# Handing out a long convolution between the steps of a Fourier layer: half-step pieces, an inverse in two channel halves, W products on every other step

## The chip, the cores and the metric

The kernel runs on one core of one Trainium2 chip. The metric is the device time of one execution in microseconds (us); smaller is better. Five engines work side by side: TensorE (PE in the profile, with its weight loads as PEld), VectorE (DVE), ScalarE (ACT), GpSimd (POOL), and SyncE (SP), which here issues DMAs and nothing else. Each engine runs its own instructions strictly in order.

## The reference

The input x has 2048 rows and 576 channels. Four layers follow each other, A, B, A, B, each added to its input:

```python
x = x + _A_ref(_layernorm(x), ...)   # FNet: y = Cr @ (n @ Wr.T) - Ci @ (n @ Wi.T)
x = x + _B_ref(_layernorm(x), ...)   # H3:   y = q * (longconv(kv, ssm_k) + kv * ssm_D)
...
```

In A, `Cr`, `Ci` are the 2048x2048 Fourier matrices of the sequence and `Wr`, `Wi` the 576x576 ones of the channels. In B, `kv` is a 4-tap convolution of k times v, `longconv` is a causal convolution of 2048 taps for each channel, done by a Fourier transform of length 4096, and q is the normalized input. So the long convolution does not depend on x: it is worked out once and used by both B layers, and until the first B needs it, it can be done at any time.

## The kernel before, in words

All products are in fp32r with three terms (high x high, high x low, low x high), so every matrix is first **split** (lines 80 to 82): ACT copies the rounded high part, DVE subtracts it for the low part.

**The main row of work** is `layer` (line 275): 128 steps of 14 matmuls of 128x512, four row blocks (tb) x real and imaginary (g) x 16 contractions (k). Each step needs one 256 KB block of the Fourier matrix (`load_c`, line 189: SP load, ACT and DVE split) and one normalized block X[k]. At the end of each g the sums are split into U (`evac_u`). When both halves of a tb are there, U times W makes eight **W products** (`hidden`, line 251: 27 matmuls of 128x288 each, two for each of four row blocks jj), handed out by `finish`. W itself is loaded and split by `load_w`, three parts a step in steps 41 to 43.

**The branch** (`branch`, line 320) is the long convolution, a generator that the main loop (lines 565 to 587) advances between steps. It has three stages:

- **f1**: 32 items; each loads a block, splits it, and does 12 matmuls of 128x288, whose results go to DRAM `t_d` by ACT's DMA queue (lines 381 to 391).
- **mid**: 64 groups (2 channel halves x 32). A group loads 288 KB of `t_d` through SP, is split (`mid_split`), has a forward product of 6 matmuls into two PSUM banks (`mid_forward`), then four ACT copies (lines 429 to 432), four DVE products and sums (lines 434 to 437), a split, and two groups later an inverse product of 3 matmuls (`mid_inverse`), one ACT copy (line 448) and a store to `v_d` (line 449).
- **i2**: 16 items of two loads of 288 KB each from `v_d`, two splits, 256 KB of constants `i2c` through POOL's DMA queue (`load_fr`, line 144), 12 matmuls for both channel halves, and a store of 288 KB to `yb_d[j]` (lines 468 to 489). It begins when all 64 groups are stored, since each item reads all of them.

The number of branch items after each step is fixed by hand: f1 until step 40, mid from step 44 to 101 (64 groups in 58 steps, about 1.1 a step), i2 from step 102 to 117 (one a step). `finish(pending, 1)` gives one W product a step from step 44. From step 118 (`PREP`) `get_x1` gates and normalizes the rows for the second A layer (it needs `yb_d[j]`). The `land` ring through which the loads of mid and i2 pass has two slots of 288 KB. The matmuls of the branch and of W share three PSUM banks (`bank`, line 66). A scheduler of the framework then fixes each engine's order from the program; an engine follows that order whatever happens on the chip.

After the 128 steps the second A layer uses a scheme of its own (Strassen, line 725), which the change doesn't touch.

Of the kernel before, what the change touches and what calls it, by code (L numbers as in the profile page):

```python
# [15 lines left out]
P = 128  # L16
S = 2048
D = 576
# [15 lines left out]
MID_END = 101  # L34
I2_END = 117
PREP = 118
MID_LAG = 2
KP = 4
# [16 lines left out]
def fnet_h3_kernel(ctx: ExitStack, tc: tile.TileContext, x, c_mat, w_re, w_im, k_pad, v, shift_k,  # L55
# [95 lines left out]
    nc.vector.memset(mhalf, -0.5)  # L151

# [25 lines left out]
    v_d = dr.tile([P, J, 2, D], F32, name="vd")  # L178
# [96 lines left out]
    def layer(get_x, xres, done, pending, blocks=TB):  # L275
        steps = [(g, tb, k) for tb in range(blocks) for g in range(2) for k in range(J)]
        for n, (g, tb, k) in enumerate(steps):
# [33 lines left out]
            yield n  # L311
# [8 lines left out]
    def branch():  # L320
# [24 lines left out]
        fcs = [None, None]  # L345

        def f1_loads(j, src):
            if fcs[0] != j:
                fc = quads(ring["fc"]())
                load_fr(fc, f1c[j])  # L350
                fcs[:] = j, fc
# [8 lines left out]
            return r, fcs[1]  # L360
# [32 lines left out]
        todo = [(j, 1) for j in range(K_FIRST)] + [(j, 0) for j in range(K_FIRST)]  # L393
# [12 lines left out]
        lay(m1, 0, ("df", 2 * D, 3), ("yf", D, 3), ("mc", 4 * P, 1))  # L406
        fresh("land")
# [6 lines left out]

        def mid_split(hf, qg):
            df = parts("df")
            d = ring["land"]()
            load_after(d, t_d[hf][4 * qg:4 * qg + 4].rearrange("q j c s d -> (q j c) (s d)"))
            split(*df, d)
            return df  # L420
# [21 lines left out]
        def mid_inverse(hf, qg, yf):  # L442
# [6 lines left out]
            nc.scalar.dma_start(v_d[4 * qg:4 * qg + 4, :, :, hf * HD:(hf + 1) * HD]  # L449
                              .rearrange("q j c d -> (q j c) d"), vo)  # L450

        dfs, yfs = [], []
        groups = [(hf, qg) for hf in range(2) for qg in range(32)]
        for n in range(len(groups) + MID_LAG + 1):
            if n >= MID_LAG + 1:
                mid_inverse(*groups[n - MID_LAG - 1], yfs.pop(0))
            if 1 <= n <= len(groups):
                yfs.append(mid_forward(dfs.pop(0)))
            if n < len(groups):
                dfs.append(mid_split(*groups[n]))  # L460
            if n < len(groups):
                yield

        fresh("fc")
        lay(m1, 0, ("vf", 2 * D, 4), ("fc", 4 * P, 2))
        lay(flts, SC_AT + 3 * NT + 2 * D, ("yo", D, 2))

        def i2_split(j):
            fc = quads(ring["fc"]())
            load_fr(fc, i2c[j])  # L470
            vf = []
            for c in range(2):
                vt = ring["land"]()
                load_after(vt, v_d[:, j, c])
                vf.append(parts("vf"))
                split(*vf[c], vt)
            return fc, vf

        def i2_products(j, fc, vf):
            yo = ring["yo"]()  # L480
            for hf in range(2):
                cs = slice(hf * HD, (hf + 1) * HD)
                ps = bank()
                for c in range(2):
                    mm(ps[:, :HD], fc[:, c, :], vf[c][0][:, cs], c == 0, False)
                    mm(ps[:, :HD], fc[:, c, :], vf[c][1][:, cs], False, False)
                    mm(ps[:, :HD], fc[:, 2 + c, :], vf[c][0][:, cs], False, c == 1)
                nc.scalar.activation(yo[:, cs], ps[:, :HD], AF.Copy)
            nc.scalar.dma_start(yb_d[j], yo)

        nxt = i2_split(0)
        for j in range(J):
            yield
            i2_products(j, *nxt)
            if j + 1 < J:
                nxt = i2_split(j + 1)
# [58 lines left out]
    load_x(0)  # L555
    load_x(1)
    for used in range(1, K_FIRST + 1):
        next(br)
        if used <= 2:
# [5 lines left out]
    for n in layer(get_x0, lambda j: x[:, j, :], done0, pending):  # L565
        if n <= F1_END:
            want = K_FIRST + (F1_16 * n // 16 if n <= 16 else F1_16 + (32 - K_FIRST - F1_16) * (n - 16) // (F1_END - 16))
        elif n <= MID_END:
            want = 33 + 64 * max(0, n - W_END) // (MID_END - W_END)
        else:  # L570
            want = min(114, 97 + 17 * (n - MID_END) // (I2_END - MID_END))
        while used < want:
            next(br, None)
            used += 1
        if F1_END < n <= W_END:
            for _ in range(3):
                next(wl, 0)
        if n >= W_SAVE and n % 2 == 0:
            next(wl, 0)
        if n > W_END:  # L580
            finish(pending, 1)
# [202 lines left out]
    for n in layer(get_x1, lambda j: xb_d[j], done1, pending, 1):  # L784
# [119 lines left out]
```

## Time and profile before

| what | value |
|---|---|
| median of 3 runs | 1252.8 us (1250.85 to 1253.81) |
| the profiled execution's own time | 1250.6 us |
| its span, first to last instruction | 1248.8 us |
| PE busy | 1195.5 us, 96% of the span, 6320 matmuls |
| DVE, ACT busy | 847.2 us (68%), 657.9 us (53%) |
| DMA | 258.29 MB, mean 207 GB/s |

How to read it: "busy" of PE counts pipelined matmuls with modelled ends, so a 128x512 matmul shows 393 ns though the next one starts much earlier. What a stretch cost beyond its matmuls is better read from start times: in steps that wait for nothing, 14 matmuls of 128x512 begin every 3.18 us (683.27 to 686.45), which is 227 ns each, and 162 matmuls of 128x288 took 21.47 us (235.20 to 256.67), which is 132 ns each. Called **lost** in this document is the time of a stretch less the number of its matmuls times these two pitches. A line in the groups view has line, engine, operation, output<-input, sizes and count, then busy time, mean ns of one, and the engine's idle time before them with what ended it.

The time lost, by stretch of the profiled execution (matmul counts from the groups of each stretch):

| us from the span's start | steps, work | matmuls 512 / 288 wide | lost |
|---|---|---|---|
| 0 to 8 | before the first matmul | 0 | 8.0 |
| 8 to 222 | steps 0 to 44, f1; W arrives | 637 / 399 | 16.7 |
| 262 to 345 | mid | 241 / 167 | 6.3 |
| 392 to 600 | mid | 506 / 606 | 13.1 |
| 600 to 680 | i2 | 180 / 169 | 16.8 |
| 680 to 800 | gate, W products of tb 3, second layer's first steps | 366 / 216 | 8.4 |

The two stretches left out between (222 to 262 and 345 to 392) lost under 1 us each; they are full of W products.

### The profile page before, as it was taken

How to read it: one execution, taken by the hardware profiler on the slowest of the kernel's cores; microseconds unless marked ns; L12 is line 12 of the kernel's file. 1: busy time of each engine (PE TensorE's matmuls, PEld its weight loads, DVE VectorE, ACT ScalarE, POOL GpSimd, SP SyncE). 2: the span in 40 equal slices, each digit the busy share in tenths (PEclk: the TensorE clock that was granted, in tenths of full speed). 3: DMA queues.
4: the chain of work that ended last, by engine and by line, in shares of the span. 5: the costliest groups of instructions: out<-in, count | busy, mean ns of one | idle time of the engine just before them, and what ended most of it. 6: DMA issues, size and time to landing. Idle time of an engine off the chain costs nothing.

```text
span 1248.8 us, 18341 instructions
## 1 busy us (share of the span) xinstructions
PE 1195.5 (96%) x6320; PEld 1027.7 (82%) x6320; DVE 847.2 (68%) x1559; ACT 657.9 (53%) x1314; POOL 76.2 (6%) x102
## 2 busy tenths in 40 slices
PE   7999999999999999999898999999999999999997
PEld 5788887888799878798777797788878878879997
DVE  7999884468854887844354974566667668775674
ACT  6865655368854887744454862544444444450220
POOL 2210000000000000000100421000000000000111
PEclk9999999999999999999999999999999999999999
DMA  9989987545565555444888883675375378787631
GB/s 320 317 249 302 274 255 222 167 128 182 179 192 164 178 144 164 134 125 126 257 259 244 295 300 130 224 254 168 117 242 190 111 255 265 256 273 225 207 134 48
DMA packets 141648, 258.29 MB, mean 207 GB/s; under 512 B 15346, under 2 KB 39922, under 8 KB 141555
## 3 DMA queue, kind: packets, MB, share of 16 engines
q1 hardware_dynamic: 102674, 205.73, 51.9%
q10 hardware_dynamic: 33984, 42.48, 9.7%
q0 software_dynamic: 4896, 8.92, 3.1%
q8 instruction: 50, 0.82, 0.3%
q14 instruction: 44, 0.35, 0.1%
HBM read 190.42 MB, written 66.65 MB: 206 GB/s over the span
## 4 chain that ended last, share of the span: by engine, by line
PE 59%; DMA 15%; DVE 11%; ACT 8%; issue 5%; POOL 2%; ACTq 0%; SPq 0%; POOLq 0%; DVEq 0%
PE s L64 31%; PE bk L64 23%; PE rm L64 5%; DMA flts<-vd 5%; DMA ph<-in_c_mat 3%; DMA t<-flts 2%; DVE mats L82 1%; ACT mid L81 1%; DMA flts<-in_c_mat 1%; DVE mid L82 1%; POOL flts L513 1%; ACT mats L81 1%; DMA xa<-flts 1%; DVE flts L373 1%; DVE ph L682 1%
## 5 line engine op out<-in xcount | busy, mean ns | idle before, releaser
L64 PE MATMUL s<-mats 128*128 128x512 f32 x2094 | 528.6, 393 | 5.4 <-DVE flts L159 2.4
L64 PEld LDWEIGHTS s<-mats 128*128 128x128 f32 x2094 | 384.6, 188 | 81.4 <-DVE mats L82 6.8
L82 DVE TENSOR_TENSOR mats<-flts,mats 128x512 fp32r<-128x512 f32 x209 | 142.8, 686 | 75.2 <-ACT mats L81 72.1
L81 ACT ACTIVATE mats<-flts 128x512 fp32r<-128x512 f32 x209 | 130.2, 626 | 116.5 <-PE rm L64 71.2
L64 PE MATMUL bk<-mid 128*128 128x288 f32 x768 | 133.4, 304 | 18.3 <-ACT mid L81 9.3
L64 PEld LDWEIGHTS bk<-mid 128*128 128x128 f32 x768 | 114.3, 188 | 44.5 <-ACT mid L81 16.6
L81 ACT ACTIVATE mid<-flts 128x576 fp32r<-128x576 f32 (+1 forms) x160 | 93.8, 588 | 88.5 <-DVE flts L437 53.4
L82 DVE TENSOR_TENSOR mid<-flts,mid 128x576 fp32r<-128x576 f32 (+1 forms) x160 | 101.8, 638 | 54.5 <-ACT mid L81 51.9
L64 PE MATMUL bk<-w,u 128*128 128x288 f32 x864 | 121.9, 296 | 4.8 <-ACT w L215 1.4
L64 PEld LDWEIGHTS bk<-w,u 128*128 128x128 f32 x864 | 117.2, 188 | 8.4 <-ACT w L215 1.8
L64 PE MATMUL rm<-mats 128*128 128x512 f32 x338 | 104.8, 390 | 0.0
L64 PE MATMUL bk<-f1r 128*128 128x288 f32 x384 | 62.6, 306 | 13.2 <-ACT f1r L81 8.0
L64 PEld LDWEIGHTS rm<-mats 128*128 128x128 f32 x338 | 63.3, 188 | 13.1
L64 PEld LDWEIGHTS bk<-f1r 128*128 128x128 f32 x384 | 57.6, 195 | 19.1 <-ACT flts L390 8.1
L160 POOL TENSOR_TENSOR flts<-flts 128x1 f32<-128x1 f32 x40 | 37.5, 938 | 519.2 <-DVE flts L159 519.2
L64 PE MATMUL s<-t,mats 128*128 128x512 f32 x258 | 64.5, 389 | 0.0
L390 ACT ACTIVATE flts<-bk 128x288 f32<-128x288 f32 x128 | 47.7, 409 | 25.0 <-DMA t<-flts 15.8
L64 PE MATMUL bk<-mats 128*128 128x288 f32 (+1 forms) x340 | 56.7, 309 | 0.0
L64 PEld LDWEIGHTS s<-t,mats 128*128 128x128 f32 x258 | 48.4, 188 | 10.1
L434 DVE TENSOR_TENSOR flts<-bk,flts 128x288 f32<-128x288 f32 x64 | 29.2, 456 | 34.1 <-ACT flts L430 33.8
L64 PEld LDWEIGHTS bk<-mats 128*128 128x128 f32 x340 | 48.8, 188 | 2.0
L64 PE MATMUL s<-mats,u 128*128 128x512 f32 x198 | 49.9, 389 | 0.0
(147 smaller groups left out, 1521.5 us busy)
## 6 DMA issues: line engine op xcount, KB each, us to landing
flts<-in_c_mat SPq DMA_DIRECT2D x150, 256.0 KB, 3.7
ph<-in_c_mat SPq DMA_DIRECT2D x48, 512.0 KB, 4.0
t<-flts ACTq DMA_DIRECT2D x64, 288.0 KB, 4.4
flts<-t SPq DMA_DIRECT2D x64, 288.0 KB, 2.9
flts<-in_c_mat SPq DMA_DIRECT2D x36, 512.0 KB, 4.9
vd<-flts ACTq DMA_DIRECT2D x64, 144.0 KB, 3.2
flts<-vd SPq DMA_DIRECT2D x32, 288.0 KB, 3.6
ud<-ph ACTq DMA_DIRECT2D x12, 512.0 KB, 4.8
```

The costliest lines, as they stand in the source:

```text
L64: nc.tensor.matmul(ps, lhsT, rhs, start=first, stop=last, skip_group_check=more)
L81: nc.scalar.activation(h, src, AF.Copy)
L82: nc.vector.tensor_tensor(l, src, h.bitcast(F32), OP.subtract)
L160: pows.append(nc.gpsimd.tensor_tensor(rs, ve, mhalf, OP.pow).ins)
L373: nc.vector.tensor_tensor(tmp if t else r, kr[j + t], w, OP.mult)
L390: nc.scalar.activation(so[:, c, :], ps[:, :HD], AF.Copy)
L434: nc.vector.tensor_tensor(p1, px[:, :HD], p1, OP.mult)
L513: pows.append(nc.gpsimd.tensor_tensor(rs, sv, mhalf, OP.pow).ins)
L682: nc.vector.tensor_tensor(src, src, r, OP.add)
```

## The change

- **Order of W products.** `finish(pending, 1)` is called on every second step instead of each (three in steps 44 to 46 as before).
- **Branch by TensorE time.** From step 44 to 111 the branch is handed out in proportion to the TensorE time of the steps (3.2 us a step, 3.6 us a W product), with each branch piece reporting a cost (0.4 and 2.7 for the two parts of a mid group, 1.2 for an i2 item; sum 236.8), and it may also be advanced in the middle of a step (`layer` yields twice). f1's last item comes one step earlier.
- **Inverse in two channel halves.** `v_d` is two tensors. i2 has 32 items of half the channels: one 288 KB load, one split, 6 matmuls, a store of 144 KB; each loads its 256 KB of `i2c` anew. The first half's items start between the groups of the second half (from group 37, every second one, until 4 are left), the other 20 come after the last group. A load is issued two items ahead and split one item ahead, where before load and split stood together.
- **Rings.** `yf` has 2 slots instead of 3; `fc` (the i2c blocks) 2 slots, and 2 more after the last group. `land` keeps its 2.
- **PREP** moves from 118 to 113.
- **First loads.** The x loads of blocks 0 and 1 are issued after the first f1 load instead of ahead of it, f1 starts with block 1 instead of block 0 (which needs `ssm_d` added), and a one-element activation comes ahead of the first wait, so that ACT's table load is not behind it.

```diff
-MID_END = 101
-I2_END = 117
-PREP = 118
+I2_END = 111
+PREP = 113
+I2_FIRST = 37
+I2_LATE = 4
+PIECE = 3.6
+STEP = 3.2
...
+    nc.scalar.activation(flts[:, 1:2], mhalf, AF.Copy)
...
+                if dc == NC // 2 - 1:
+                    yield n, False
...
-        todo = [(j, 1) for j in range(K_FIRST)] + [(j, 0) for j in range(K_FIRST)]
+        todo = [(j, 1) for j in reversed(range(K_FIRST))] + [(j, 0) for j in range(K_FIRST)]
...
-        lay(m1, 0, ("df", 2 * D, 3), ("yf", D, 3), ("mc", 4 * P, 1))
-        fresh("land")
+        at = lay(m1, 0, ("df", 2 * D, 3), ("mc", 4 * P, 1))
+        fresh("land", "fc")
+        spare = at
+        at = lay(m1, at, ("yf", D, 2))
+        lay(m1, at, ("fc", 4 * P, 2))
...
+        def i2_products(hf, j, fc, vf):
+            yo = ring["vo"]()
+            ps = bank()
             for c in range(2):
+                cs = slice(c * HD, (c + 1) * HD)
+                mm(ps[:, :HD], fc[:, c, :], vf[0][:, cs], c == 0, False)
+                mm(ps[:, :HD], fc[:, c, :], vf[1][:, cs], False, False)
+                mm(ps[:, :HD], fc[:, 2 + c, :], vf[0][:, cs], False, c == 1)
+            nc.scalar.activation(yo, ps[:, :HD], AF.Copy)
+            nc.scalar.dma_start(yb_d[j][:, hf * HD:(hf + 1) * HD], yo)
+
+        mids = [(0, hf, qg) for hf in range(2) for qg in range(32)]
+        late = [(1, 0, j) for j in range(J)]
+        feeds = []
+        for g, f in enumerate(mids):
+            feeds.append(f)
+            if g >= I2_FIRST and (g - I2_FIRST) % 2 == 0 and len(late) > I2_LATE:
+                feeds.append(late.pop(0))
+        feeds += late + [(1, 1, j) for j in range(J)]
...
+        for i, (kind, hf, q) in enumerate(feeds):
+            df, fc = halves.pop(i)
+            if kind:
+                i2_products(hf, q, fc, df)
+            else:
+                if len(yfs) == MID_LAG:
+                    mid_inverse(*yfs.pop(0))
+                    yield 0.4
+                yfs.append((hf, q, mid_forward(df)))
+            split_feed(i + 1)
+            load_feed(i + 2)
...
+            yield 1.2 if kind else 2.7
...
-    load_x(0)
-    load_x(1)
     for used in range(1, K_FIRST + 1):
         next(br)
+        load_x(used - 1)
...
+    def pieces(n):
+        if n < 2 * J + J:
+            return (n > W_END) * (1 if n < 3 * J - 1 else 2 * TB - (3 * J - 2 - W_END))
+        return int(n % (2 * J) < J and n % 2 == 1)
+
+    for n in range(W_END + 1, I2_END + 1):
+        total += STEP + PIECE * pieces(n)
+        paced.append(total)
+    work = 64 * 3.1 + 32 * 1.2
...
+        if n > W_END:
+            if whole and pieces(n):
+                finish(pending, 1)
+            m = n - W_END - 1
+            if m + 1 < len(paced):
+                done_by = paced[m] + (paced[m + 1] - paced[m] if whole else STEP * 3 / 7)
+            else:
+                done_by = total
+            while spent < work * done_by / total:
+                spent += next(br, work)
```

Where the work stands on TensorE in each program's own order (S is a main step of 14 matmuls, a W product has 27, branch matmuls are counted):

| steps | before | after |
|---|---|---|
| 41, 42 | f1: 24, 12 | f1: 36, 0 |
| 44 to 46 | W products in 45 and 46, first mid in 46 | S alone |
| 47 | mid 6, six W products in a row | mid 48 and eight W products, the last five in a row, at the end |
| 48 to 52 | mid 9 a step | mid 18, 18, 12, 15, 18 |
| 53 to 65 | mid 9 a step, more in 54, 64 and 65 | mid 3 to 9 a step, mean 7 |
| W products of tb 1, tb 2 | 65 to 71 in a row, 96 to 103 | 66 to 78 every second step and 79; 98 to 110 every second step and 111 |
| i2 | all from 102 to 118 | 12 half items from 76 to 102, 4 in 107, the second half's 16 in 108 to 112: 4, 2, 5, 2, 3 |

More of the change, by code (lines that the diff above doesn't have):

```diff
@@ L448, in mid_inverse @@
             nc.scalar.activation(vo, pv[:, :HD], AF.Copy)
[L449 to L471, printed above, removed]
-            for c in range(2):
[L473 to L489, printed above, removed]
@@ new lines, in split_feed @@
+        def split_feed(i):
+            if i < len(feeds):
+                d, fc = landed.pop(i)
+                df = parts("df")
+                split(*df, d)
+                halves[i] = df, fc
+        load_feed(0)
+        load_feed(1)
+        split_feed(0)
+        for i, (kind, hf, q) in enumerate(feeds):
+            df, fc = halves.pop(i)
+            if kind:
+                i2_products(hf, q, fc, df)
[6 more added lines that the diff above has]
+            load_feed(i + 2)
+            if i == last_mid:
+                while yfs:
+                    yield 0.4
+                    mid_inverse(*yfs.pop(0))
+                old = ring["fc"]
+                held = [old.tiles[(old.n + m) % 2] for m in range(2)]
+                fresh("fc")
+                lay(m1, spare, ("fc", 4 * P, 2))
+                ring["fc"].tiles.extend(held)
+            yield 1.2 if kind else 2.7
@@ L783, in fnet_h3_kernel @@
     loaded, builds = [], []
-    for n in layer(get_x1, lambda j: xb_d[j], done1, pending, 1):
+    for n, whole in layer(get_x1, lambda j: xb_d[j], done1, pending, 1):
+        if not whole:
+            continue
         finish(pending, 1)
```

63 lines of the change are left out of this document (31 added, 32 removed).

## Prediction, made before the changed kernel was run

> **What bounds the kernel now.** I read the engine shares first: TensorE is busy almost all the time, so only the time lost between its matmuls can be won. Then I took each stretch's matmuls by the groups view and subtracted them at 227 and 132 ns, as the table above does: 62 us are lost between 8 and 800 us, where the change works, and 8.0 us before the first matmul. Third, the busy time by stretch:
>
> ```profile
> PE 1195.5 (96%) x6320; PEld 1027.7 (82%) x6320; DVE 847.2 (68%) x1559; ACT 657.9 (53%) x1314; POOL 76.2 (6%) x102
> ```
> ```profile
> 262.00:345.00 83.00, 79.84 (x408) 66.88 (x407) 67.27 (x133) 68.48 (x152) 0.00 (x0) 1.00 0.58 176
> 355.00:390.00 35.00, 35.00 (x225) 32.70 (x224) 17.35 (x35) 17.78 (x39) 0.00 (x0) 1.00 0.54 168
> ...
> 600.00:680.00 80.00, 70.72 (x349) 55.94 (x348) 32.03 (x46) 38.21 (x76) 6.89 (x13) 0.98 0.85 253
> 680.00:710.00 30.00, 29.14 (x127) 23.25 (x126) 26.76 (x79) 21.32 (x44) 11.78 (x13) 1.00 0.87 289
> ```
>
> Columns: stretch, length, busy us of PE, PEld, DVE, ACT, POOL, granted clock, DMA share, GB/s. With a mid group in each step (262 to 345) ACT and DVE are busy 82%; with W products beside it (355 to 390) only 50%, and TensorE loses nothing. In i2 (600 to 680) ACT and DVE are idle half the time and TensorE still loses 16.8 of 80 us. The waits and the chain of that stretch say why:
>
> ```profile
> PE bk L64 <- ACT mid L81: 8.1, 9, 1.7
> ```
> ```profile
> ACT mid L81 <- DMA flts<-vd: 24.9, 21, 3.2
> ```
> ```profile
> 657.27 4.59 DMA flts<-vd
> 661.95 0.69 ACT mid L81
> 662.67 0.77 DVE mid L82
> 663.45 3.17 DMA flts<-vd
> 666.71 0.69 ACT mid L81
> 667.42 0.77 DVE mid L82
> ```
>
> The chain is a closed loop: a load lands, ACT and DVE split it, the slot is free, the next load starts. Each turn serves both slots of `land`; 30 loads were issued in 593.1 to 670.2, so a load per 2.7 us, whatever TensorE does.
>
> **The change, part by part.** Matmuls are the same 6320; only lost time moves.
>
> *Start.* Now TensorE starts at 7.97, behind ACT's table load (5.94 to 7.22), which waited for the third DMA. With the table early and the f1 block first, its landing is that of the first x load (issued 0.74, used 3.83), then a split of 0.68: first matmul near 4.6. But the steps need X[0], whose chain (statistics, POOL, two ACT passes) ended at 13.97 and shrinks by about 1 us, with 24 instead of 21 matmuls done before it (0.4 us). I take -1.5; bounds -3.4 (all of it) and +1 (x later, since its load is behind).
>
> *End of f1 and W.* 36 f1 matmuls in step 41 instead of 24 and 12: TensorE has 7.9 us there, while six result pairs must leave by three buffers at 0.8 us of ACT copies and a 4.4 us store, two turns of 5.2 us: +1, bounds 0 and +2.5. Before, W products in steps 45 and 46 waited 3.1 us for W (216 to 223). W's loads reuse f1's buffers, so they follow f1's end; W was complete 16.7 us after it (206.98 to 223.7), the mid constants 19. In the new order 16.8 us of steps lie between, so 1 to 2 us of wait stay: -1.6, bounds -3.1 and +1.
>
> *Mid.* A group costs ACT 0.68 + 4 x 0.40 + 0.45 + 0.41 = 3.15 us and the step's own split 0.62. In runs of one group a step the period was 4.64 us (the groups at 316.16, 320.80, 325.44) where TensorE has 4.37, so 0.25 us is lost each; where two groups fell into a step, another 0.8 to 1.5. That is 20.3 us from 222 to 600. The new pace spreads 236.8 of branch cost, 76 groups' worth, over 68 steps x 3.2 + 24 W products x 3.6 = 304 us: (304 + 76 x 1.19) / 76 = 5.2 us for a group, 12% above the period. But the order starts late: 9 groups stand in steps 48 to 52, where TensorE has 5 x 3.18 + 81 x 0.132 = 26.6 us. ACT needs 9 x 3.15 + 5 x 0.62 = 31.5 us (4.9 lost); at the period it is 41.8 us (15.2 lost). I take 6, four extra groups at the 1.4 us that an extra one cost, nearer to ACT's own bound. Steps 53 to 106 have some ten with 15 to 21 branch matmuls, which I put at 0.6 each, under the 0.8 above since most have a W product or a half step between: 6. Together 12 for 20.3: -8.3, bounds -14 and +1.
>
> *i2.* The first 16 half items' loads stand at most one to a step in SP's order, their landing is 3.6 us: I cost them at nothing, as they land in the shade of a step's matmuls. The last 16 are in five steps whose matmuls need 31.7 us from the first item to the start of the last (five steps, two of three W products). Their loads still pass two slots: at 5.4 us for two, items 15 and 16 come 7 x 5.4 = 37.8 us after the first; TensorE wants item 15 at 30.1: 7.7 lost. Before the first of them the last inverse must be stored and read back: 0.4 + 3.2 + 3.6 + 0.7 us and issue, about 9, covered by 9.9 us of other matmuls. I take 8 for 16.8: -8.8, bounds -13 and 0.
> The i2c blocks are loaded twice, 4.2 MB more. The tail moves 16 x 0.70 MB, six steps' blocks and rows, about 14.6 MB in 42 us of matmuls. The stretch 600 to 680 ran at 253 GB/s with the DMA engines 85% busy, so about 298 is the cap by this row: 49 us, 6.5 lost, not on top of the loop's 7.7 but at the same loads. The Trainium skill (DMA: Bandwidth & Descriptors, Specifications) gives about 358 GB/s for a core's HBM; by it the bytes would need an estimated 41 us and this second limit would be gone, leaving the sum as it is. The highest slice of this trace is 320 GB/s, so the row stands and the rival of the starved tail keeps its chance.
>
> *Second layer's gate.* From 690 to 720 DVE is busy 96% with `get_x1` (about 4.1 us of DVE per row) and 3.3 us are lost; from 770 to 800 another 5.0, as one row's statistics wait for its reloaded sum (idle 4.15 us of DVE ahead of 777.05) with the steps' splits behind them. Starting at 113 leaves 15 bare steps (48 us) instead of 9 for twelve rows; the first loss goes, the last rows' chain stays: -4, bounds -7 and 0. SP's queue is the same in kind: Fourier blocks are issued four to five steps ahead in both orders, which covers the five `v_d` loads that stand between two of them.
>
> **Sum:** -1.5 + 1 - 1.6 - 8.3 - 8.8 - 4 = -23 from the profiled execution's 1250.6 (2.2 below the median of the three): **1228 us**.
>
> **The rivals.**
> *Dense restart:* steps 48 to 52 run at the group period, 9 more: 1237. For: the copies, sums and splits of a group stand in order on ACT and DVE. Against: the two engines could overlap two groups.
> *Starved tail:* with 16 more i2c loads a landing is 5.2 us, as the f1c loads had in the crowded f1 stage, instead of 3.9: two slots turn in 6.7, item 15 comes at 47 us, i2 wins nothing: 1237. Both rivals: 1246.
> *Slower:* the half items stand in TensorE's order, each behind its own fresh `v_d` load and i2c block, with the next mid group behind it. If all 32 wait s, it is 1228 - 8 + 32s: level with before at s = 0.95 us, 1258 at 1.2, the longest single wait being 1.7. Against: loads go out two items ahead, and ACT is idle half the time there.
> *W products don't spread:* eight in step 47 already show that the order doesn't follow the call; this is in the sum.
>
> A second rule: the trace has granted clock 0.85 and 0.73 in 672 to 676 and 676 to 680, after 4 us in which TensorE was busy 2.69. The Trainium skill (TensorE: Matmul & The Clock Gate, What's actually happening) halves the clock after an idle window of about 3.4 us; here no wait was longer than 1.7, so partly idle is enough. In the new tail such a dip costs about 1.7 us, half of 3.4, inside i2's bounds.
>
> **How the numbers follow.** Forecast (1218 to 1234) 0.52; dense restart 0.17; starved tail 0.12; both 0.06; slower 0.08; better than 1218, most bounds at their good end, 0.05. Eight in ten: 1217 to 1245, which leaves out the slower case, the better one and part of "both". A difference under 0.2% (2.5 us) can't be told from none. Faster 0.88 (all but the slower case and two thirds of "both"), same 0.04, slower 0.08.
>
> **What would show it.** First matmul near 4.6; no W wait over 2 us before step 47; waits of TensorE on ACT L433 or L449 in the stretch of steps 48 to 52 (about 6 us; 15 is the first rival); in the tail a closed loop of `vd` loads with 8 us lost; DVE under 90% just after it; a layer 2 start with the last 4 us still lost. Wrong would be: mid stretches that lose as much as before, or waits ahead of single i2 items between mid groups.

## The result and the profile after

The changed kernel takes 1243.5 us (median of 8 runs, 1240.3 to 1247.4) beside 1251.4 us of the kernel before (8 runs on the same chip, 1245.6 to 1257.5): ratio 0.9938, 95% interval 0.9912 to 0.9964. Run again later beside the kernel before it had 0.9957 (0.9933 to 0.9982). So it is faster by 5 to 8 us, not by the 23 that I forecast; the time lies at the upper end of my range. The profiled execution of the changed kernel took 1246.3 us, with a span of 1244.5.

The engine shares of the changed kernel:

```profile
PE 1192.8 (96%) x6320; PEld 1031.2 (83%) x6320; DVE 847.5 (68%) x1559; ACT 658.4 (53%) x1315; POOL 81.5 (7%) x116
```

The work of DVE and ACT is what it was. The busy time by stretch, the same four stretches and columns as before:

```profile
262.00:345.00 83.00, 82.49 (x436) 69.92 (x435) 66.58 (x132) 67.32 (x149) 0.00 (x0) 1.00 0.60 178
355.00:390.00 35.00, 35.00 (x210) 31.40 (x209) 22.62 (x46) 22.70 (x52) 0.00 (x0) 1.00 0.55 170
600.00:680.00 80.00, 68.84 (x356) 57.74 (x356) 40.21 (x88) 40.13 (x80) 14.75 (x23) 0.96 0.86 266
680.00:710.00 30.00, 27.96 (x126) 21.94 (x125) 26.20 (x78) 23.84 (x49) 9.98 (x14) 1.00 0.88 286
```

ACT and DVE are as busy between 262 and 345 as before (81%), but the mean hides two parts. In the crowded steps 48 to 52 (268.8 to 296.2 us) ACT is busy 25.9 of 27.4 us; behind them (296.2 to 337.8) it is busy 31.1 of 41.5 us, 75%. The inverse's tail (600 to 680), of which the forecast expected most, has TensorE busy 68.84 us; before it was 70.72.

What TensorE and then ACT wait for in the tail (line, releaser, us in all, times, longest):

```profile
PE bk L67 <- ACT mid L84: 4.9, 3, 2.6
PE bk L67 <- ACT flts L460: 2.3, 2, 1.2
PE bk L67 <- DMA mid<-in_i2c: 1.7, 1, 1.7
```
```profile
ACT mid L84 <- DMA flts<-vd: 18.0, 8, 3.2
ACT flts L460 <- DMA yb<-flts: 6.8, 5, 2.2
ACT flts L460 <- DMA vd<-flts: 3.5, 1, 3.5
```

The first line of each is the old wait, now 18.0 us in 8 waits. In the kernel before, the same 80 us have 24.1 us in 19 waits (the prediction's 24.9 in 21 are of 596 to 682), so the waits are fewer and longer. Two are new: the i2c block, and the output copy L460, which waits until an earlier store from its ring of two slots has landed. The chain of the tail, in order of time:

```profile
602.76 5.17 DMA yb<-flts
...
610.37 5.82 DMA flts<-vd
616.23 0.04 issue
616.27 0.69 ACT mid L84
...
626.18 5.03 DMA flts<-vd
631.25 0.04 issue
631.30 0.69 ACT mid L84
632.02 0.77 DVE mid L85
632.80 5.05 DMA flts<-vd
...
637.97 3.93 DMA yb<-flts
```

The closed loop of before is on it, with landings of 5.0 to 5.8 us where 3.2 to 4.6 stood, and stores to `yb` stand beside it. The landings on the chain are the longest ones: the median of the `vd` loads issued from 600 to 680 us is 3.6 us in both kernels.

**Lost time** (as in the prediction: the stretch less its matmuls at 227 and 132 ns; us), with a second profile of each of the two kernels, taken with the experiments:

| stretch | before | changed | difference of the means | forecast |
|---|---|---|---|---|
| up to 200, with the start | 22.4, 20.7 | 23.6, 22.8 | +1.6 | -0.5 |
| 200 to 600 (W, mid) | 24.7, 25.9 | 21.9, 22.9 | -2.9 | -9.9 |
| 600 to 680 (tail of i2) | 17.2, 15.4 | 16.9, 16.4 | +0.4 | -8.8 |
| 680 to 800 (second layer's gate) | 8.8, 6.5 | 5.0, 4.6 | -2.9 | -4 |
| behind 800 | 8.0, 8.4 | 8.7, 9.0 | +0.6 | 0 |

They sum to -3.2, of which 0.8 comes back behind the last matmul (6.5 us to the end of the span before, 7.3 after). The medians say -5 to -8. The profiled executions were 1250.6 and 1246.4 us of before and 1246.3 and 1246.0 of the changed kernel, 2.3 apart in the mean, so some 3 to 6 us of the gain in the medians do not show in these four profiles, and I can't place them. Runs of one kernel spread widely (the changed kernel's second set: 1237.0 to 1253.1).

### The profile page after: what moved, and what is told of

Read it like the earlier page. It is cut to its first block, busy times and chain, and to the rows that moved or that the text cites. A ratio compares the mean times of both kernels' runs of the same rounds, so it can differ in the third digit from the quotient of the medians.

```text
span 1244.5 us, 18406 instructions
## 1 busy us (share of the span) xinstructions
PE 1192.8 (96%) x6320; PEld 1031.2 (83%) x6320; DVE 847.5 (68%) x1559; ACT 658.4 (53%) x1315; POOL 81.5 (7%) x116
## 4 chain that ended last, share of the span: by engine, by line
PE 67%; DMA 14%; DVE 9%; ACT 6%; issue 3%; POOL 1%; SPq 0%; ACTq 0%; POOLq 0%; DVEq 0%
PE s L67 35%; PE bk L67 27%; PE rm L67 5%; DMA ph<-in_c_mat 2%; DMA flts<-in_c_mat 2%; DVE mats L85 1%; DMA flts<-vd 1%; DMA t<-flts 1%; ACT mats L84 1%; DMA vd<-flts 1%; DMA yb<-flts 1%; DVE ph L720 1%; DVE mid L85 1%; DMA gate<-xa 1%; ACT mid L84 1%
## 5 line engine op out<-in xcount | busy, mean ns | idle before, releaser
L67 PE MATMUL bk<-mid 128*128 128x288 f32 x768 | 128.4, 303 | 16.8 <-ACT mid L84 4.9
L67 PEld LDWEIGHTS rm<-mats 128*128 128x128 f32 x338 | 63.5, 188 | 15.4 <-issue 2.3
L67 PEld LDWEIGHTS bk<-f1r 128*128 128x128 f32 x384 | 57.8, 196 | 17.8 <-ACT flts L395 7.0
L395 ACT ACTIVATE flts<-bk 128x288 f32<-128x288 f32 x128 | 48.1, 409 | 23.4 <-DMA t<-flts 12.6
L67 PEld LDWEIGHTS s<-t,mats 128*128 128x128 f32 x258 | 48.4, 188 | 10.1
```

The costliest lines, as they stand in the source:

```text
L67: nc.tensor.matmul(ps, lhsT, rhs, start=first, stop=last, skip_group_check=more)
L395: nc.scalar.activation(so[:, c, :], ps[:, :HD], AF.Copy)
```

## Experiments

All start from the changed kernel, unless said. The columns are lost us in one profile each, in the stretches above; "ratio" is to the kernel before, timed on the same chip. The two theories I began with: the tail of i2 is held by its load loop or by the loads that were doubled; the mid stage by ACT's load per group or by something that load does not measure.

| run | to 200 | 200-600 | 600-680 | 680-800 | ratio (95%) |
|---|---|---|---|---|---|
| again | 22.8 | 22.9 | 16.4 | 4.6 | 0.9957 (0.9933-0.9982) |
| vo6 | 23.4 | 21.5 | 16.5 | 5.4 | 0.9966 (0.9949-0.9983) |
| land4 | 21.9 | 23.6 | 11.0 | 8.8 | 0.9949 (0.9924-0.9974) |
| fconce | 23.5 | 22.9 | 10.1 | 3.4 | 0.9881 (0.9850-0.9912) |
| share4 | 23.7 | 23.0 | 15.2 | 4.6 | 0.9970 (0.9953-0.9986) |
| i2late | 25.7 | 20.6 | 15.8 | 8.1 | 0.9939 (0.9920-0.9959) |
| prep118 | 21.3 | 24.0 | 14.3 | 11.1 | 0.9979 (0.9961-0.9997) |
| kk2 | 22.8 | 15.0 | 11.7 | 4.3 | 0.9864 (0.9825-0.9902) |
| kk2pad | 22.9 | 16.2 | 11.7 | 4.9 | 0.9879 (0.9850-0.9908) |
| poolkk | 24.3 | 22.0 | 14.8 | 4.1 | 0.9914 (0.9889-0.9939) |
| poolkk2 | 21.9 | 29.8 | 17.9 | 6.2 | 1.0028 (1.0011-1.0045) |
| whole | 23.6 | 24.5 | 14.6 | 7.8 | 0.9988 (0.9968-1.0007) |
| wdense | 22.5 | 25.2 | 18.4 | 6.0 | 0.9969 (0.9946-0.9993) |
| mcfirst | 25.1 | 23.3 | 17.8 | 4.6 | 0.9969 (0.9948-0.9989) |
| oldstart | 22.5 | 20.4 | 13.3 | 3.7 | 0.9956 (0.9934-0.9978) |
| best | 23.0 | 19.7 | 18.0 | 4.1 | 0.9955 (0.9937-0.9973) |
| pool2land4 | 21.3 | 32.1 | 13.4 | 10.1 | 1.0057 (1.0036-1.0077) |
| befagain (before) | 20.7 | 25.9 | 15.4 | 6.5 | 1.0002 (0.9983-1.0020) |

The rows give the spread too: with the same code from 200 to 600 us, that stretch lost 20.4 to 24.0. A stretch runs from the first matmul that starts in it to the first of the next stretch, so a wait across a bound moves 1 to 2 us from one column to the next. Where that matters, losses below are counted between two matmuls of the same number, or from the first matmul of one step to that of another.

### The tail of i2

**vo6**, a larger store ring from the last group on:

```diff
+                fresh("vo")
+                lay(flts, SC_AT + 3 * NT + 2 * D, ("vo", HD, 4))
+                ring["vo"].tiles.extend(held)
```

> The changed kernel with four more slots in the ring of output copies from the last mid group on (from the free kk space), so that an i2 copy need not wait until an earlier yb store has landed. In the changed kernel 16.9 us are lost from 600 to 680 us, and ACT waits 4.6 us there for yb stores and 3.5 for a vd store. Theory A (the two-slot load loop bounds the tail): ACT's wait for stores goes, its wait for vd loads grows instead, and 600 to 680 keeps 14 to 17 us lost. Theory B (the shared store ring is what undid the gain): 600 to 680 falls to 9 to 11 us lost and the kernel by 6 us. Theory C (i2c traffic): as A.

The copy's wait for the stores was gone, ACT's wait for `vd` loads grew from 18.0 to 22.6 us, and the stretch lost 16.5. The store ring, although it stands among the waits, held nothing that the stretch or the ratio shows.

**land4**, four load slots and loads four items ahead:

```diff
+                lay(flts, SC_AT + 3 * NT + 2 * D, ("land", D, 2))
+                ring["land"].tiles.extend(held)
+                load_feed(i + 3)
+            if i >= last_mid:
+                load_feed(i + 4)
```

> The changed kernel with four land slots instead of two from the last mid group on, and loads issued four items ahead instead of two; nothing else. Theory A (two-slot load loop): ACT's 18 us of waiting for vd loads falls to under 8, and 600 to 680 from 16.9 to about 8 us lost, the kernel by 8 us. Theory B (store ring): the wait moves to the yb stores, 600 to 680 keeps 13 to 16. Theory C (the doubled i2c traffic, DMA full): landings of vd and i2c loads grow by what the loads are issued earlier, 600 to 680 keeps 13 to 17.

ACT's waits from 600 to 680 in this run:

```profile
ACT flts L460 <- DMA yb<-flts: 17.6, 13, 3.0
ACT mid L84 <- DMA flts<-vd: 5.9, 3, 2.8
```

The wait for loads went to 5.9, as the two-slot theory said, and the stretch to 11.0 us. But the `vd` landing grew from 3.6 to 5.8 us (median), the i2c landing from 5.2 to 6.0, the stores became the wait (17.6), and 680 to 800 lost 8.8 instead of 5.0. The landings grew as the traffic theory said. The sum of all losses was 75.7, beside 76.1 and 75.7 in the two profiles of the changed kernel, and the ratio did not move. Slots win in the tail what is then lost behind it.

**fconce**, twelve of the second i2c loads left out:

```diff
-                    load_fr(fc, i2c[q])
+                    if hf == 0 or q < 4:
+                        load_fr(fc, i2c[q])
```

> The changed kernel without twelve of the sixteen second loads of the i2c blocks: the second channel half of blocks 4 to 15 is multiplied by blocks that are already in the buffer, so this part of the computation is changed; 3.1 MB less are read, the matmuls, copies and other loads are all there. Theory C (starved tail, the doubled i2c loads): vd landings fall from about 5 us to under 4, no i2c wait is left and 600 to 680 falls from 16.9 to about 9. Theory A (two slots): landings fall by 0.5 to 1 us at most and 600 to 680 keeps 13 to 16. Theory B: as A.

```profile
ACT mid L84 <- DMA flts<-vd: 11.9, 8, 2.8
```

ACT's wait for the loads fell from 18.0 to 11.9 with as many waits, the `vd` landing to 3.1, and the stretch to 10.1. Profiles whose tail has the same code lost 13.3 to 17.9, and 11.7 where the tail starts earlier (kk2, kk2pad); between the same two matmuls it is 9.1 against 13.9 to 17.7. TensorE's own wait for an i2c block stayed (1.8), so the gain came through the landings of the other loads. A part of it is the clock: from 600 to 680 it was granted at 1.00 here and at 0.94 to 0.98 in the others, which is an estimated 1.6 to 4.8 us at most (the share of 80 us that is missing), and whether the waits bring it about no run separates. With 0.9881 it is the fastest but for the two with a shorter mid group. Theory C held, but for the i2c wait, which it had gone.

**share4** keeps four blocks for the second half, with the result the same:

```diff
-        feeds += late + [(1, 1, j) for j in range(J)]
+        feeds += late + [(1, 1, j) for j in (*range(J - I2_LATE, J), *range(J - I2_LATE))]
...
+                    fc = kept.pop(q, None) if hf else None
+                    if fc is None:
```

> The changed kernel with the last four blocks of the first channel half kept for the second: the second half's blocks come in the order 12 to 15, then 0 to 11, so that four of the 32 i2c loads (1.0 MB, all in the tail) are left out and the result is the same. Twelve loads less took the loss from 600 to 680 us to 10.0 from 13.3 to 18.4 in the profiles whose tail has the same code. If it goes with the bytes, four loads less win about 2 us: 12 to 15.5 there, kernel 1 to 3 us faster than the changed one. Rival (only the last loads count, or the first wait after the last mid group): 15 to 18, no difference in the time.

15.2 us, inside the spread, and no faster. **i2late** spreads the items over three more steps:

```diff
-I2_END = 111
-PREP = 113
+I2_END = 114
+PREP = 116
```

> The changed kernel with the branch work's end at step 114 instead of 111 and the second layer's preparation at 116 instead of 113: the last items, with the same loads, are spread over three more steps. If the tail loses time because its loads (i2c twice, vd, the steps' own) come faster than the memory gives, 600 to 680 falls from 16.9 to 9 to 13 us, and 680 to 800 grows from 5.0 to 7 to 9 since the preparation has three steps less: the kernel within 3 us of the changed one. Rival (each item's wait is its own, whatever the density): 600 to 700 loses as much as before, only later, and the kernel is 3 to 5 us slower than the changed one.

15.8 us there and 8.1 behind: the loss did not thin out with the density, and only the gate's part came as said. So the loss does not go simply with bytes per time: twelve loads less win 6 us, four less or a thinner spread nothing that can be told. The rows say why I would not call it bandwidth. In land4 eight slices of 1.5 us in a row (612 to 624) moved 361 to 408 GB/s, above the 298 that I had taken for the cap, yet the mean from 600 to 660 was 297, and 267 in the changed kernel. I read that as short bursts, in which each landing waits for the others, and pauses in which the slots wait for a split; no run shows it alone.

**prep118**:

```diff
-PREP = 113
+PREP = 118
```

> The changed kernel with the second layer's preparation started at step 118 again, as before the change, instead of 113; nothing else. If the earlier start is what took the loss between 680 and 800 us from 8.6 to 5.0 us, it returns: 8 to 9 us lost there and the kernel slower by 3 to 4 us. Rival (the gain came from the branch work that ends earlier, and the start of the preparation is only a bound): 680 to 800 stays at 4 to 6 and the time within 1 us; the tail, with no second-layer rows beside it, may then lose 1 to 2 us less.

The loss is back: 11.1 against 5.0 and 4.6, 10.5 of it from 680 to 725 us, ratio 0.9979. The earlier start is worth 6 us by the stretch, 3 to 5 by the ratios.

### The mid stage

**kk2**, two copies for four:

```diff
-            nc.scalar.activation(kk[lo, 0, :], pk[lo, :HD], AF.Copy)
-            nc.scalar.activation(kk[hi, 0, :], pk[lo, :HD], AF.Copy)
-            nc.scalar.activation(kk[lo, 1, :], pk[hi, :HD], AF.Copy)
-            nc.scalar.activation(kk[hi, 1, :], pk[hi, :HD], AF.Copy, scale=-1.0)
+            nc.scalar.activation(kk[:, 0, :], pk[:, :HD], AF.Copy)
+            nc.scalar.activation(kk[:, 1, :], pk[:, :HD], AF.Copy)
```

> The changed kernel with two copies in place of four in each mid group, so that the halves of the second factor are not exchanged and the sign is not turned (this part of the computation is changed); ACT's work per group falls by 0.8 of 3.15 us, and the chain from forward to inverse is shorter by as much. Theory M1 (TensorE's losses from 200 to 600 us are waits for ACT's and DVE's work per group): they fall from 21.5 to 24.0 us to 13 to 16, above all in steps 48 to 52. Theory M2 (most of the loss is a fixed cost that each hand-over has, whatever the engines' load): 200 to 600 stays at 19 to 23.

This kernel leaves out the exchange of the halves and the sign, so its result is another. 15.0 us: M1, it seemed. But the gain was not where M1 had most of it: steps 48 to 52 lost 2.3 us, and 2.4 in the changed kernel. And the copies also stand in a row that TensorE waits for. A stretch of the changed kernel's chain of waits, where a group is late, shows it:

```profile
285.79 0.40 ACT flts L431
...
286.22 0.29 ACT flts L432
...
286.55 0.45 ACT mid L84
...
287.03 0.46 DVE mid L85
...
287.52 0.46 DVE flts L436
...
288.00 0.45 DVE flts L437
```

The copies of one group, the split of the group ahead of it, then the products: one engine after the other, 0.01 to 0.04 us apart, and TensorE's next products need the banks and the parts at its end. I measured this row as the time from a group's first copy to the end of its sum on DVE, the median of the 64 groups; what the two engines do for others in between is in it. **kk2pad** puts load back on ACT behind this row:

```diff
+            for i in range(4):
+                nc.scalar.activation(flts[:, 2 + i:3 + i], p1[:, i:i + 1], AF.Copy)
```

> As the run with two copies in place of four (the same part of the computation is changed), with four one-element copies on ACT behind each mid group's split, about 0.2 us each by the one that the profile shows: ACT's load per group is back at about 3.15 us, but the added work lies behind the group's own chain. If TensorE waits for ACT's load as such (the queue behind a group is late for the next split), 200 to 600 us is back at 20 to 24 us lost. If it waits for the length of the chain from the forward products to the inverse, it stays at 14 to 17. In between says both.

16.2 us, so the chain.

**poolkk** takes load off ACT:

```diff
-            nc.scalar.activation(kk[hi, 0, :], pk[lo, :HD], AF.Copy)
+            nc.gpsimd.tensor_copy(kk[hi, 0, :], kk[lo, 0, :])
```

> The changed kernel with one of ACT's four copies in each mid group (lower to upper half of the first plane) done by POOL out of the copy that ACT has just made; the values are the same. ACT's work per group falls from 3.15 to 2.75 us. If ACT's work per group is what TensorE waits for (two copies less took the loss from 200 to 600 us from 21.5 to 24 down to 15.0), it falls to 18 to 20 here, and the kernel by 3 us. Rival (POOL's copy is longer than the 0.40 us of ACT's and lies on the chain to the product, or slows DVE beside it): 200 to 600 loses 22 to 27.

22.0 us in the stretch, the lower end of the rival; ratio 0.9914.

**poolkk2** takes off the second such copy as well:

```diff
-            nc.scalar.activation(kk[hi, 1, :], pk[hi, :HD], AF.Copy, scale=-1.0)
+            nc.gpsimd.tensor_scalar(kk[hi, 1, :], kk[lo, 1, :], -1.0, None, op0=OP.mult)
```

> The changed kernel with both upper-half copies of a mid group done by POOL from the lower halves that ACT has just made (one as it is, one times -1); the values are the same. ACT's load per group falls to 2.35 us as in the runs with two copies, and the chain becomes ACT 0.40, ACT 0.40, then POOL about 0.48 for the last, 1.3 us instead of 1.6, and the bank of the first products is free after 0.8 instead of 1.6. If TensorE waits for the chain and the bank (two copies less: 15.0 us lost from 200 to 600, with 0.47 us of load put back behind it 16.2; one copy moved to POOL with the chain as long: 22.0): 200 to 600 falls to 16 to 19 and the ratio to the kernel before is 0.986 to 0.991. Rival (POOL's work beside DVE makes DVE slower, or POOL stands behind its DMA issues for the i2c blocks): 20 to 24 and 0.991 to 0.996.

It missed by far, and tells load and row apart. Its POOL rows from 200 to 680, and its busy time (ACT is the fourth engine number):

```profile
L433 POOL TENSOR_SCALAR flts<-flts 64x288 f32<-64x288 f32 x64 | 63.4, 991 | 1.9
L431 POOL COPY flts<-flts 64x288 f32<-64x288 f32 x64 | 30.3, 474 | 251.1 <-issue 162.4 <-ACT flts L430 85.3 <-DVE mid L85 3.2
```
```profile
262.00:345.00 83.00, 78.90 (x396) 64.05 (x395) 62.54 (x120) 47.80 (x106) 27.38 (x34) 1.00 0.55 164
```

POOL needs 991 ns for the multiply, twice its copy and 2.5 times ACT's: the row got longer while ACT got idle. (The Trainium skill, GPSIMD Engine Reference, Engine selection, has POOL near line rate for operations of one input and about twice as slow for two, beside VectorE. The copy agrees, 474 ns beside 459 of DVE's product L436 of the same size and ACT's 403; the multiply by a constant does not.) The rival has a share in it: from 262 to 345 us DVE's sum L438 took 535 ns, and 452 in the changed kernel. That time is part of the row.

| kernel | ACT busy in 262-345, of 83 us | first copy to sum, us | lost 200-600, us | lost in steps 53 to 106, us |
|---|---|---|---|---|
| kk2 | 52.0 | 3.03 | 15.0 | 6.4 |
| kk2pad | 58.0 | 3.04 | 16.2 | 5.6 |
| poolkk | 59.1 | 3.54 | 22.0 | 9.9 |
| changed | 67.3 | 3.79 | 21.9 | 13.8 |
| poolkk2 | 47.8 | 4.06 | 29.8 | 19.6 |

The loss follows the third column, not the second. poolkk2 has the least load and the greatest loss; kk2pad had 60% of kk2's saving back (0.47 of 0.8 us) and lost no more than kk2: the 1.2 us between them in the fourth column are the bound's, between the same two matmuls they lost 12.3 and 12.2. Two pairs have the same load and another row: kk2 and poolkk2 (0.81 us of ACT copies a group), kk2pad and poolkk (1.28 and 1.22 us). poolkk shows its gain in the last column alone, where other profiles of the changed kernel's mid code had 11.1 to 15.0; it gave 1.2 us back in steps 48 to 52 (3.6 for 2.4). In those crowded steps the row does not explain the loss, since kk2 won nothing there. Whether TensorE waits for the banks that the row holds or for the parts at its end, I did not separate.

**pool2land4** (poolkk2 with land4's slots), whose base had fallen:

> The same POOL copies, and the four load slots with loads four items ahead in the tail, of which the tail won 5 us and the stretch behind it gave back 4. If the tail is held by its load slots once the mid groups are faster: 600 to 680 loses 7 to 10 and the ratio is 0.003 below that of the run without them. If the memory's share is what is left (twelve i2c loads less won 6 us, four won nothing that could be told): the gain of the tail is given back between 680 and 800 again and the ratio is within 0.002.

Ratio 1.0057, 0.003 above poolkk2. The tail won 4.5 us and 680 to 800 gave back 3.9: land4 once more.

**whole** hands out work at whole steps only, behind the W product:

```diff
+        if not whole:
+            continue
         if n > W_END:
-            if whole and pieces(n):
-                finish(pending, 1)
...
                 spent += next(br, work)
-        if not whole:
-            continue
+            if pieces(n):
+                finish(pending, 1)
```

> The changed kernel with branch work handed out at whole steps only (after the W product of the step), not at half steps; pace, spread of W products, the inverse in halves and the loads are as in the changed kernel. If the half steps win time: 200 to 600 us loses 3 to 6 us more than the 21.5 to 24.0 of the changed kernel's code, and 600 to 680 as much as 17 or more. Rival (a half step only changes the place of a group, its waits come with it): both stretches stay within 1.5 us and the kernel within 2 us.

Lost 24.5 in the mid stage and 7.8 at the gate, ratio 0.9988, so 4 to 6 us slower than the changed kernel by the ratios. The stretches show neither theory: 24.5 is 0.5 above the changed kernel's range, and the tail lost 14.6 where 17 or more was expected. The interval (0.9968 to 1.0007) lies clear of the changed kernel's first one and overlaps the second, so that the half steps are worth most of what the change won is likely and not shown.

**wdense** undoes the spread of W products:

```diff
-        return int(n % (2 * J) < J and n % 2 == 1)
+        return int(n % (2 * J) < 2 * TB)
```

> The changed kernel with its W products in eight steps running again, one a step from each block's first step, and the branch pace worked out for that; half steps, the inverse in halves and the loads are as in the changed kernel. If the spread of the W products wins time in the mid stage, 200 to 600 us loses 3 to 5 us more than the 21.5 to 24.0 of the changed kernel's code, in the steps without a W product. Rival (the pace by TensorE time alone does it, or nothing does): it stays within 1.5 us.

25.2 us and 0.9969: 2 to 3 us more in the stretch than the changed kernel's two profiles and 1.2 above the range, a little under what was expected; the intervals of the ratios overlap.

**mcfirst** loads the mid constants ahead of W's:

```diff
         nc.scalar.activation(mc, quads(raw), AF.Copy)
+        yield
...
             if n == F1_END:
                 next(br)
+                next(br)
```

> The changed kernel with the mid constants loaded and copied ahead of W's loads at the end of f1, where the changed kernel loads them behind all nine; nothing else is changed in the code. In five profiles with the same code up to step 75 the stretch from 200 to 600 us lost 21.5 to 24.0 us, 2.3 of it the first mid group's wait for the constants. Theory (the wait for W that went has only become a wait for the mid constants behind it in SP's queue): that wait goes, groups start one or two steps earlier, 200 to 600 falls by 2 to 4. Rival (the loads as a whole are late, whichever comes first): W products wait 2 to 3 us again and 200 to 600 stays at 21.5 to 24.

The wait for the constants went, and W products waited again (0.88, 0.66, 0.61 and 0.53 us lost at 221 to 228): 23.3, the rival. The loads are late as a whole.

### The start, and the parts together

**oldstart** issues the x loads first again:

```diff
+    load_x(0)
+    load_x(1)
     for used in range(1, K_FIRST + 1):
         next(br)
-        load_x(used - 1)
```

> The changed kernel with the two x loads issued first again, ahead of the f1 rows; the early table load and the order of the f1 blocks stay. Up to 60 us the changed kernel loses 16.5 us in its profile (5.95 to the first matmul, which is the landing of the f1c block, 6.7 among the first 24 f1 products, 1.9 until X[0] is ready, 1.9 after). Theory (the start of the steps is set by X[0], whose load, and the statistics behind it, now come later): the first matmul stays near 6, X[0] is ready 1 to 2 us earlier and the first 60 us lose 14 to 15.5. Rival (the first f1 products and the Fourier splits on ACT set it, not x): 16 to 17.5 as in the changed kernel.

What TensorE waits for up to 16.5 us in the changed kernel:

```profile
PE bk L67 <- DMA f1r<-in_f1c: 6.0, 1, 6.0
PE s L67 <- ACT mats L175: 1.9, 1, 1.9
PE bk L67 <- ACT f1r L84: 1.5, 1, 1.5
```

The second line is X[0]; the steps start at 15.86 us with it, and at 14.98 in oldstart, 0.9 earlier and not 1 to 2. Its first matmul did not stay near 6: the f1 row, now behind x, had it wait until 8.19. That run lost 14.7 up to 60 us (best, with the same start, 15.1), against 15.5 to 20.8 with the changed order; up to 200 us it lost 22.5, as others did, and the ratio is the same. A gain at the start that is not kept.

**best** has oldstart, poolkk and share4:

> The changed kernel with three things together that leave the result as it is: x loads first again at the start, POOL's copy in the mid groups, and the four shared i2c blocks. The first two had ratios of 0.9956 and 0.9914 beside 0.9957 of the changed kernel on the same chip. If they add up by the stretches (about 2 us at the start, 3 to 4 in the mid groups' longer waits, 2 in the tail): 0.987 to 0.991. If what one stretch wins the next gives back, as with the four load slots: 0.991 to 0.996.

0.9955: they do not add up. The mid stage had 19.7, the tail 18.0. The best kernel with the result kept is poolkk, 0.9914, surely faster than before; that it beats the changed kernel (0.9957 on the same chip) the intervals leave just open, and best, which has its copy, did not. **again** and **befagain** are the unedited kernels:

> The changed kernel once more, unedited, to have it beside the others on the same chip and to see how far the stretches of two profiles of one kernel lie apart: ratio 0.991 to 0.997 to the kernel before; 200 to 600 us loses 21.5 to 24, 600 to 680 15 to 18, 680 to 800 4 to 6, and the first 60 us 16 to 18 with the wait for the first matmul.

> The kernel before once more, unedited, for the spread of its stretches: ratio 1.000 within 0.002; lost 200 to 600 us 23 to 26 (24.7 in its first profile), 600 to 680 16 to 18.5, 680 to 800 7.5 to 9.5, first 60 us with the start 15 to 17.5. If 200 to 600 falls under 22.5, the mid stage's difference between the two kernels is within what two profiles of one kernel differ by.

The ranges held but for the changed kernel's start (18.4, expected up to 18) and two of before (gate 6.5 and tail 15.4, both lower). The mid stage's 25.9 keeps the difference there real.

## Why the prediction failed

The sum failed in three terms: the tail of i2, which won nothing, steps 53 to 106 of the mid stage, which lost more than twice what I put, and W. That the time came near the 1246 of both rivals together is luck: only one of the two showed.

- **i2** failed whole, in "Their loads still pass two slots: at 5.4 us for two". That took the landing of before, 3.9 us, and put the doubled i2c loads beside it as a limit of bytes, "not on top of the loop's 7.7 but at the same loads". They came on top: landings on the chain are 5.0 to 5.8, close to the 5.2 of the rival *starved tail*, to which I gave 0.12, and as it said the tail won nothing. The median landing of a `vd` load stayed at 3.6; the loop pays for the long ones. fconce, without twelve of these loads, lost 6 to 7 us less than the changed kernel's two profiles, the clock's part included. Since four loads less and a thinner spread won nothing, how the loss goes with the loads stays open.
- **Mid** failed in "5.2 us for a group, 12% above the period". The average has that slack, but it comes as steps with little or no group; where groups come together, the row of copies, products and sum is as long as it was (3.78 us before, 3.79 after), and TensorE waits for it. Nor is 4.64 us a fixed period: in the kernel before, steps 47 to 51 had one group each, took 4.4 us and lost 0.05 us or less. By steps, in two profiles of each kernel (us lost):

| steps | before | changed | forecast |
|---|---|---|---|
| 48 to 52 | 0.4, 0.3 | 2.4, 2.4 | 6 |
| 53 to 106 (before: with the first i2 items) | 21.9, 21.8 | 13.8, 13.0 | 6 |
| of these, 53 to 62 | 3.4, 3.4 | 0.2, 0.2 | |
| of these, 63 to 66 and 96, 97 | 4.8, 4.8 | 6.6, 6.3 | no term |

The rival *dense restart* (15 us in steps 48 to 52) was no cause, and my 6 there was too much. The term that was too small is "some ten with 15 to 21 branch matmuls", 6 us for steps 53 to 106. Where the groups are even, the pace won nearly all (53 to 62). Half of what is left lies where one row block ends and the next begins, and for that the sum had no term. The two longest single waits of the changed kernel from 200 to 600 us are for the mid constants and for the addition that reads a block's remainder sums out of their bank (`evac_r`):

```profile
PE bk L67 <- ACT mid L420: 2.3, 1, 2.3
PE rm L67 <- DVE flts L252: 1.9, 1, 1.9
```

With kk2's shorter row steps 53 to 106 lost 6.4. From 226.5 to 585 us, waits over 0.8 us fell from 8.1 to 3.4 us (7 to 2 of them), those of 0.3 to 0.8 rose from 4.0 to 5.5 (8 to 12), and those under 0.3 from 5.7 to 6.4. The pace broke long waits into short ones, and I had let the short ones go for nothing.

- **W**: the 3.1 us of waits for W went, and 2.3 came back as the first group's wait for the mid constants behind W's loads. I had said 1 to 2 us would stay, on W: -0.8 for -1.6. By steps nothing was won: 44 to 47 lost 3.9 us in both profiles of before, and 5.1 and 6.5 in the changed kernel, which has 60 branch matmuls there instead of 21.
- **Start**: the early table load uncovered the f1c block (first matmul at 5.95, not 4.6), and X[0], now loaded behind, set the steps at 15.86 instead of 14.13 (15.45 and 15.18 in the second profiles). Nothing won for -1.5; the bound of +1 was the better guide. The end of f1 was costed at +1 and is within the spread (195 to 210 us: 0.6 lost in both profiles of before, 0.5 and 1.1 after).
- **Gate**: -4 was near in size (-2.9 by the profiles, 6 us back in prep118). But I had it in the wrong place: the loss of the last rows went (725 to 800: 5.2 and 2.6 before, 0.2 and 0.1 after), and that beside busy DVE stayed (680 to 725: 3.6 and 3.9, then 4.9 and 4.4). The earlier start of the rows is not what took the last rows' loss away: with the start at 118 again it stayed at 0.6, and 680 to 725 lost 10.5. So the start keeps the loss beside DVE from growing, and which part of the change freed the last rows no run separates.
- The clock dip that I priced came in the tail as said: granted clock 0.50 from 615 to 620 us, in which TensorE was busy 2.99 of 5 (2.74 of 5 in the five before), and TensorE's longest wait from 600 to 680 was 2.6 us. (In the kernel before, the 2.69 of 4 us that I set ahead of the dip are of 672 to 676, in which it began; 670 to 674 had 2.17.) One that I had not priced stands at the change of row block in the first profile (0.91 from 340 to 350 and 0.92 from 350 to 360, with TensorE busy 8.06 of the first ten) and not in the second, which lost 3.6 us in steps 63 to 66 instead of 4.7.

## What to carry over

Where an engine hands a group to two others and back, sum the row of operations that it waits for; an average load with slack says nothing about it, and moving work to an idle engine lengthens the row if that engine is slower. Where groups, block ends and other work meet, count the loss step by step, and give the meetings a term of their own. Work that is split in two loads its shared operands twice: cost that as longer landings of the loads that something waits for, on top of a slot loop, not as a separate limit of bytes. A wait taken away at one place uncovers the load that was hidden behind it (the f1c block, the mid constants), so name the second latest before you book the gain.

## What the runs showed of the hardware

- POOL's multiply by a constant on 64x288 took 991 ns, its copy 474 (poolkk2).
- The matmul after a waiting one loses about 0.11 us as well (median behind the changed kernel's 50 waits over 0.3 us), so a wait costs a little more than its length. That its weights (189 ns to load) were not fetched ahead is my reading, not tested.
- 1.5 us slices reach 408 GB/s (land4). The Trainium skill (HBM Reference, Specifications) gives about 358 GB/s as a core's share and about 425 for a core that streams alone; this trace agrees with the second, and in the prediction I had weighed only the first. The 320 GB/s that I called the highest slice there is the mean of 31 us; in 2 us slices from 600 to 680 the kernel before had already reached 367.
- The landing of the first f1c block moved the first matmul between 5.3 and 7.7 us from profile to profile of the same code.
